# Gated linear attention and hard-swish layer: weight loads on one queue, and another written order of all steps

## The chip, the core and the metric

The kernel runs on one core of a Trainium2 chip. Its time is the device time of one launch in microseconds (us). The times of the kernel before are the median of seven runs; its profile is of one further look at one of these executions, recorded by the hardware profiler.

## The reference

Two blocks are computed one after the other, all in float32 on the chip. The inputs of the second block arrive as float64; the kernel gets their bits and rounds them itself.

```python
# attention: batch 4, heads 8, sequence 768, head size 48
for t in range(S):
    state = alpha[:, :, t, :, None] * state + einsum('bhd,bhe->bhde', k[:, :, t], v[:, :, t])
    y[:, :, t] = einsum('bhd,bhde->bhe', q[:, :, t], state)
# feed forward: x is y as (3072 tokens, 384), w_in (384, 2048), w_out (2048, 384)
h = x @ w_in
g = h * clip(h + 3, 0, 6) / 6
out = g @ w_out
```

## The kernel before

**Tiling.** The 3072 tokens are cut into 24 chunks of 128 tokens (six for each batch), and the chunks are taken in pairs, so there are 12 groups of 256 tokens. The attention of a chunk needs the state that the chunk before has left; the feed-forward part of a group needs the attention of its two chunks. The first two groups (0 and 1) use plain products for the first layer, and group 0 for the second layer too. All other products are done with a scheme of Strassen's kind that needs fewer multiplications: sums of weights are made once on VectorE, sums of activations for each group.

**Weights.** Each matrix is cut into eight slices: 0 to 7 of `w_in`, 8 to 15 of `w_out`. A slice of 768 KB of float64 bits lands in a raw buffer (`load_weight`, L170 to L188; a slice of `w_in` by four transfers of 192 KB, L184, a slice of `w_out` by one, L187). Then five steps make float32 of it: `round_low` (L207, ScalarE), `magnitude` (L217, ScalarE), for slices 0, 1, 2 and 4 also `sign` (L212, ScalarE), `high_bits` (VectorE, L224 and L226 for these slices, L228, L229 and L231 for the others), and `add_low` (L238, GpSimd). Slices share three raw buffers (slices 3 and 4 have room elsewhere), so a later load waits for the `add_low` of an earlier slice.

**Order.** Nothing is scheduled by a tool at build time: the order is written out by hand as one list of 1665 words (the string passed to `run`, L842 on, inside `manual_schedule`). A word such as `sc.1.1.2` calls one step, with the chunk or group first and the PSUM banks to use last. Each engine takes its own instructions strictly in the order of this list, and SyncE its transfers. An instruction that waits holds up all that follow on its engine. The words that matter here:

- `la`, `lk`, `lq`, `lv`: loads of one chunk of alpha, k, q, v, issued by SyncE (L273, L303 and L304 for the first six or eight chunks, as 192 KB and two times 96 KB).
- `w`: `load_weight`; `d1`, `d2`, `dx`, `d3`, `d4`: `round_low`, `magnitude`, `sign`, `high_bits`, `add_low`.
- `ta`, `tk`, `tq` (L314): transposes on TensorE; `ca` (L332, ScalarE) places alpha; `r` (L341, L345) and `p` (L352) are the scans on VectorE; `k`, `q` (L364) the scalings on VectorE.
- `sc` (L408): scores on TensorE; `m` (L416): mask on VectorE; `kb` (L428) and `ck` (L437, ScalarE): k by token; `u` (L494): state update on TensorE; `sm` (L507, L509, VectorE) and `st` (L471, GpSimd): next state; `yi` (L539) and `yx` (L549): the chunk's output on TensorE; `cy` (L557, ScalarE) keeps it.
- `fa`, `fb` (L582): a slice of the first layer for one of the two chunks of group 0; `f` (L571): for a whole group; `fr` (L587, ScalarE) and `fg` (L591, VectorE): its hard swish; `b` (L609): a quarter of the second layer for a chunk of group 0.
- `M` (L693), `n` (L699, ScalarE), `o` (L630 to L634, VectorE), `e` (L587, ScalarE), `h` (L591, VectorE): a product of the first layer, its copy, the sums, and hard swish, from group 2 on. `P` (L796): a product of the second layer, from group 1 on; `s` (L740, L757, VectorE) its sums, `K` (L775), `G` (L809 and L812), `O` (L817) its copies, outputs and stores. `y`, `x`, `xc`: sums of weights and of activations on VectorE.
- `z` (L625): matmuls of the identity into a bank that nobody reads; 29 of them stand in the opening.

**Semaphores of transfers.** The framework gives eight semaphores in turn to the transfers that SyncE and ScalarE issue, so a transfer waits for the landing of the one eight places before it.

The choice of the queue in `load_weight`:

```python
queue = nc.scalar if i < 5 and p > 1 else nc.sync
queue.dma_start(out=to[32 * p : 32 * p + 32], in_=src[p])
```

Of the kernel before, what the change touches and what calls it, by code (L numbers as in the profile page):

```python
# [17 lines left out]
def kernel(  # L18
# [32 lines left out]
    nc = tc.nc  # L51
# [9 lines left out]
    G = 2  # L61
# [66 lines left out]
    st, sm = [], []  # L128
# [43 lines left out]
    def load_weight(i):  # L172
        u = 2 if wide else 1
        dst = weight_dst(i)
        m = dst.shape[1]
        to = raw_of(i).rearrange("p (m n) w -> p m (n w)", m=m) if wide else dst
        if i < NW1:
            n = NSL // KT
            src = moe_w_in[:, u * i * n : u * (i + 1) * n].rearrange(
                "(p t r) f -> p r t f", p=NP, t=KT)  # L180

            for p in range(NP):
                queue = nc.scalar if i < 5 and p > 1 else nc.sync
                queue.dma_start(out=to[32 * p : 32 * p + 32], in_=src[p])  # L184
        else:
            o = (i - NW1) * m * C
            nc.sync.dma_start(  # L187
                out=to, in_=moe_w_out[o : o + m * C, :].rearrange("(f p) n -> p f n", p=C))  # L188
# [476 lines left out]
    for i in range(8):  # L665
        r, o = divmod(i, 3)
# [174 lines left out]
    with tc.manual_schedule():  # L841
        run("""la.0 z.3.5 lv.0.0 lk.1 lq.0 ta.0.0 lv.1.1 z.0.3 ca.0 r.0 lk.0 tk.1.1 la.1 p.0 tq.0.2  # L842
               z.0.8 la.2 q.0 lq.1 tk.0.3 z.0.2 k.0 lv.3.2 ta.1.0 sc.0.2.3 ca.1 la.3 r.1 ta.2.0 w.1
               z.0.3 ca.2 m.0 kb.0.0 z.0.2 ck.0 r.2 tq.1.2 yi.0.3 p.1 z.0.3 lq.2 cy.0 k.1 u.0.0 q.1
               lk.2 ta.3.3 sm.0 sc.1.1.2 ca.3 lk.3 p.2 d1.1 kb.1.0 w.0 m.1 st.1 d2.1 tq.2.3 dx.1
               z.0.1 q.2 yi.1.1 d3.1 tk.2.2 ck.1 yx.1 r.3 u.1.3 lq.3 cy.1 k.2 d4.1 tk.3.0 lv.2.0
               sm.1 sc.2.1.2 k.3 w.3 st.2 fa.1.0 d2.0 m.2 d1.0 kb.2.3 d3.0 fb.1 dx.0 p.3 tq.3.0 w.4
               z.1.2 ck.2 d4.0 q.3 fr.0.1.0 u.2.1 sc.3.2.3 fg.0.1 sm.2 fa.0.1 m.3 st.3 d2.3 d1.3
               kb.3.0 w.5 d3.3 fb.0 ck.3 u.3.1 fr.0.0.1 yi.3.2 d4.3 sm.3 d1.4 fg.0.0 yi.2.3 d2.4 w.2
               dx.4 yx.3 d3.4 yx.2 f.0.3.2 cy.3 d4.4 cy.2 d1.5 la.5 d2.5 f.1.3.3 fr.0.3.0 lq.5 d3.5  # L850
               la.4 d1.2 f.1.4.0 fg.0.3 lv.4.1 d4.5 d2.2 dx.2 w.6 d3.2 tq.5.0 fr.1.3.1 ta.4.1 d4.2
               fr.1.4.0 ta.5.2 fg.1.3 fa.4.1 ca.4 fg.1.4 ca.5 r.4 w.7 fa.2.2 r.5 f.0.5.3 p.4 d2.6
               d1.6 st.4 lq.4 fb.2 fr.0.5.1 d3.6 w.8 f.1.5.0 fr.0.2.0 d1.7 fg.0.5 d4.6 fg.0.2 d2.7
               tq.4.3 fr.1.5.1 f.1.0.3 d3.7 w.9 q.4 d4.7 f.1.6.2 fr.1.0.0 fg.1.5 d2.8 fg.1.0 p.5
               d1.8 w.10 f.1.7.0 d3.8 fr.1.6.1 d2.9 q.5 f.0.7.3 d4.8 d1.9 lk.4 fg.1.6 fr.1.7.0 d3.9
               w.11 f.0.6.2 fr.0.7.1 d2.10 fg.1.7 d4.9 d1.10 fg.0.7 tk.4.1 fr.0.6.0 d3.10 f.1.2.0
               w.12 k.4 d4.10 fb.4 fg.0.6 d2.11 fr.1.2.1 d3.11 sc.4.2.3 w.13 d1.11 fr.0.4.0 f.1.1.3
               fg.0.4 d4.11 m.4 d2.12 d1.12 kb.4.0 lk.5 d3.12 b.1.0.2 fr.1.1.0 ck.4 w.14 fg.1.1
               d4.12 d2.13 fg.1.2 b.0.0.1 d1.13 d3.13 w.15 u.4.1 tk.5.2 d4.13 sm.4 b.1.1 k.5 d2.14
               st.5 d1.14 d3.14 lq.6 sc.5.3.0 yi.4.1 m.5 lq.7 d4.14 b.1.2 d2.15 d1.15 d3.15 la.6  # L860
               yx.4 b.0.1 tq.6 d4.15 lv.5.2 y.6 la.7 b.1.3 y.5 y.1 y.7 lk.7 y.2 y.11 yi.5.2 bo.1 x.0
               so.1 b.0.2 lv.7.0 y.4 y.13 ca.6 yx.5 y.0 b.0.3 cy.5 r.6 la.8 y.3 x.1 s.1.0.0 P.1.0.3
               P.1.1.0 lv.9.1 s.1.1.1 P.1.3.2 cy.4 xc.2.0 s.1.3.2 x.2 s.1.2.3 s.1.4 s.1.5 y.8 xc.2.1
               y.16 K.1.0 P.1.2 bo.0 K.1.2 K.1.1 M.2.15.1 M.2.16 x.3 P.1.4 P.1.5 y.10 y.12 y.9
               xc.2.3 y.15 G.1.1.0 P.1.6 G.1.3.1 xc.2.4 tk.7 lk.9 lk.6 xc.2.5 y.17 xc.2.7 G.1.0.2
               y.19 y.20 xc.2.6 M.2.7.0 n.2.7.8 y.18 M.2.0.3 xc.2.8 M.2.8 G.1.2.3 y.21 y.23 n.2.0.9
               M.2.1 n.2.1.10 o.2.4.0 M.2.17 M.2.2 n.2.2.11 xc.2.9 M.2.18.2 M.2.3 M.2.4 p.6 tk.6 q.6
               ca.7 lq.8 la.9 lv.6.2 lk.8 k.6 sc.6.0.3 xc.2.10 r.7 k.7 xc.2.2 n.2.4.12 o.2.0.0 p.7
               M.2.5 M.2.9 kb.6.2 kb.7.1 n.2.18.13 e.2.0.0 ck.7 tq.7 lq.9 M.2.19 o.2.1.0 M.2.10
               u.7.1 ck.6 u.6.2 O.1.3 m.6 yi.6.0 q.7 y.14 n.2.10.14 sm.6 h.2.0 o.2.5.0 y.22 M.2.11  # L870
               n.2.11.15 o.2.7.0 e.2.5.1 h.2.5 y.24 cy.6 sc.7.3.2 m.7 M.2.12 n.2.12.12 st.7 e.2.1.0
               h.2.1 o.2.6.0 M.2.6.2 e.2.4.1 M.2.13 xc.3.0 n.2.5.14 o.2.3.0 n.2.13.11 o.2.2.0 yi.7.0
               yx.7 cy.7 xc.3.1 xc.3.2 xc.3.3 o.2.2.1 e.2.2.0 M.2.14 xc.3.4 P.2.0.3 o.2.7.1 xc.3.5
               o.2.3.1 M.3.0.1 n.3.0.13 xc.3.7 M.3.7.2 xc.3.6 h.2.4 o.2.6.1 h.2.2 e.2.3.1 h.2.3
               e.2.6.0 M.3.1 P.2.1.0 n.3.7.12 K.2.0 ca.8 tk.8 xc.3.10 xc.3.8 h.2.6 G.2.0.1 n.3.1.11
               e.2.7.1 M.3.2 M.3.8 h.2.7 s.2.0.8 r.8 s.2.1.10 s.2.2.14 k.8 n.3.2.9 M.3.3 M.3.4
               n.3.4.15 o.3.0.0 P.2.3.0 kt.8 s.2.3.8 M.3.5 M.3.9 p.8 lv.10.2 lv.8.0 vh.8 P.2.2
               o.3.1.0 tq.8 s.2.5 q.8 xc.3.9 tk.9 ca.9 M.3.10 K.2.2 P.2.5 n.3.5.10 e.3.0.0 e.3.1.1
               O.1.2 O.1.0 kw.8 lk.10 kr.8 sm.7 r.9 st.8 sc.8.2.3 m.8 s.2.4 h.3.0 K.2.1 n.3.10.8
               M.3.11 M.3.15.1 M.3.16 n.3.11.14 yi.8.0 O.1.1 yx.8 lq.10 la.10 tq.9 lq.11 G.2.2.3  # L880
               O.2.2 k.9 p.9 u.8.1 M.3.12 sm.8 kt.9 kw.9 q.9 h.3.1 M.3.18.0 n.3.18.15 P.2.4 G.2.1.2
               ca.10 sc.9.2.3 m.9 M.3.19 o.3.5.0 n.3.12.9 vh.9 M.3.13 st.9 yi.9.1 yx.9 o.3.4.0
               e.3.4.0 o.3.3.0 M.3.6.0 n.3.13.9 M.3.14 tk.10 o.3.2.0 cy.8 cy.9 xc.4.1 o.3.3.1 xc.4.3
               o.3.2.1 xc.4.4 o.3.6.0 P.2.6 G.2.3.0 vh.10 M.3.17 e.3.2.1 xc.4.5 r.10 xc.4.6 tq.10
               p.10 M.4.0.0 n.4.0.9 P.3.0.3 K.3.0 O.2.1 la.12 kr.9 lv.13.0 lk.11 la.11 xc.4.0 k.10
               q.10 M.4.1 u.9.2 o.3.7.0 o.3.6.1 xc.4.7 xc.4.8 h.3.2 sc.10.3.0 m.10 xc.4.2 h.3.4
               o.3.7.1 ca.11 M.4.7.2 n.4.1.15 e.3.6.1 M.4.2 n.4.2.11 yi.10.1 M.4.3 M.4.4 n.4.7.12
               M.4.8 e.3.5.0 h.3.5 e.3.3.0 n.4.4.8 r.11 h.3.3 P.3.1.1 M.4.5 h.3.6 s.3.0.13 o.4.0.0
# [123 lines left out]
```

## Time and profile before

| what | value |
|---|---|
| median of 7 runs | 547.97 us (547.51 to 551.35) |
| the profiled execution's own time | 549.09 us |
| its span, first to last instruction | 547.3 us |
| granted TensorE clock | 0.999 |
| TensorE matmul, busy | 538.9 us (98%) |
| TensorE weight load, busy | 512.0 us (94%) |
| VectorE, busy | 470.5 us (86%) |
| ScalarE, busy | 203.9 us (37%) |
| GpSimd, busy | 55.6 us (10%) |
| HBM read and written | 43.71 MB and 8.13 MB |
| loads of `w_in` on ScalarE's queue | 10 of 192 KB, median 6.0 us to landing |

The busy time of TensorE bridges short waits, since the ends of matmuls are modelled. Whether it waits is seen in the starts of its instructions: within one kind they follow each other at a fixed distance (a matmul of 128x192 every 163 ns, of 128x128 every 112 ns, of 128x256 every 217 ns), and what exceeds that is lost. The times of single steps below are starts of their first instruction, taken from the timeline by counting the words of the list.

### The profile page before, as it was taken

The page shows a single profiled execution, that of the slowest core. Times are in us where ns is not written, and L with a number is a line of the kernel's source. Part 1 is how long each engine was busy: PE and PEld are TensorE (multiplying, and loading weights), DVE is VectorE, ACT ScalarE, POOL GpSimd, SP SyncE. Part 2 cuts the span into 40 slices and gives each one's busy share as a digit, 9 for nine tenths or more (in the row PEclk, how much of TensorE's full clock was granted, in tenths as well). Part 3 has the DMA queues.
Part 4 walks back from the last instruction along what each step waited for, and adds up shares of the span by engine and source line. Part 5 has one row for each costly group of instructions (what it writes and reads, how often), then busy time and mean ns, then how long its engine had stood idle before and what let it go on. Part 6 is the DMA issues. An engine that isn't in the chain of part 4 may idle for free.

```text
span 547.3 us, 14906 instructions
## 1 busy us (share of the span) xinstructions
PE 538.9 (98%) x6222; PEld 512.0 (94%) x6222; DVE 470.5 (86%) x822; ACT 203.9 (37%) x358; POOL 55.6 (10%) x76
## 2 busy tenths in 40 slices
PE   8999999999999999999999999999999999999996
PEld 8789886699999999999999999999999999999996
DVE  6978997989999999999999998999999796375571
ACT  2487663002543242241432443333243333333330
POOL 3334336000001000000100000000100100000000
PEclk9999999999999999999999999999999999999999
DMA  8998678204414442542443542245143300000000
GB/s 181 193 202 174 207 230 220 63 9 104 94 29 126 111 104 66 140 123 71 126 118 84 151 101 59 79 107 141 38 116 86 91 23 2 1 23 2 23 14 30
DMA packets 98515, 52.82 MB, mean 97 GB/s; under 512 B 51472, under 2 KB 91664, under 8 KB 98448
## 3 DMA queue, kind: packets, MB, share of 16 engines
q1 hardware_dynamic: 97328, 49.91, 36.2%
q10 hardware_dynamic: 1120, 1.97, 1.7%
q8 instruction: 49, 0.80, 0.6%
q14 instruction: 18, 0.15, 0.1%
HBM read 43.71 MB, written 8.13 MB: 95 GB/s over the span
## 4 chain that ended last, share of the span: by engine, by line
PE 94%; issue 2%; DMA 1%; DVE 1%; ACT 1%; ACTq 0%; POOL 0%; POOLq 0%
PE m_ps L796 35%; PE m_ps L693 34%; PE m_ps L571 6%; PE m_ps L609 4%; PE t_ps L549 2%; PE t_ps L383 2%; PE t_ps L529 2%; PE m_ps L582 2%; DMA v<-in_v_dram 1%; PE t_ps L533 1%; PE t_ps L408 1%; PE t_ps L314 1%; PE m_ps L625 1%; PE t_ps L539 1%; PE t_ps L488 1%
## 5 line engine op out<-in xcount | busy, mean ns | idle before, releaser
L796 PE MATMUL m_ps<-w,g_sb 128*128 128x192 f32 x704 | 121.3, 326 | 0.0
L699 ACT COPY g_sb<-m_ps 128x512 f32<-128x512 f32 x110 | 63.5, 585 | 142.8 <-PE m_ps L693 127.9
L796 PEld LDWEIGHTS m_ps<-w,g_sb 128*128 128x128 f32 x704 | 113.8, 190 | 0.4
L796 PE MATMUL m_ps<-rings,g_sb 128*128 128x192 f32 x528 | 91.4, 326 | 0.0
L796 PEld LDWEIGHTS m_ps<-rings,g_sb 128*128 128x128 f32 x528 | 85.4, 190 | 0.1
L693 PE MATMUL m_ps<-xc,w 128*128 128x128 f32 x640 | 82.7, 277 | 0.0
L693 PEld LDWEIGHTS m_ps<-xc,w 128*128 128x128 f32 x640 | 77.9, 192 | 1.6 <-issue 1.2
L587 ACT ACTIVATE r<-g_sb,half 128x512 f32<-128x512 f32 x80 | 56.6, 721 | 40.5 <-DVE g_sb L634 16.1
L591 DVE SCALAR_TENSOR_TENSOR g_sb<-r,g_sb 128x512 f32<-128x512 f32 x80 | 54.4, 693 | 8.1 <-ACT r L587 5.5
L471 POOL TENSOR_TENSOR t<-t,R 128x384 f32<-128x384 f32 x20 | 21.2, 1059 | 337.8 <-DVE t L509 128.7
L693 PE MATMUL m_ps<-xT,raw 128*128 128x128 f32 x400 | 52.3, 277 | 0.0
L693 PEld LDWEIGHTS m_ps<-xT,raw 128*128 128x128 f32 x400 | 48.7, 192 | 0.5
L740 DVE TENSOR_TENSOR g_sb<-g_sb 128x512 f32<-128x512 f32 (+1 forms) x55 | 42.5, 799 | 3.5 <-PE m_ps L796 3.2
L693 PE MATMUL m_ps<-xT,w 128*128 128x128 f32 x320 | 42.6, 277 | 0.0
L693 PEld LDWEIGHTS m_ps<-xT,w 128*128 128x128 f32 x320 | 39.4, 192 | 0.6 <-issue 0.2
L571 PE MATMUL m_ps<-xT,w 128*128 128x256 f32 x144 | 32.3, 381 | 0.0
L693 PE MATMUL m_ps<-xc,raw 128*128 128x128 f32 x240 | 32.1, 277 | 0.0
L341 DVE TENSOR_TENSOR_SCAN R<-t,ones 128x516 f32<-128x516 f32 x24 | 29.9, 1246 | 2.1 <-ACT t L332 2.0
L571 PEld LDWEIGHTS m_ps<-xT,w 128*128 128x128 f32 x144 | 26.9, 190 | 3.7 <-issue 0.2
L630 DVE TENSOR_TENSOR g_sb<-m_ps,g_sb 128x512 f32<-128x512 f32 x30 | 20.5, 683 | 11.3 <-ACT g_sb L699 8.8
L693 PEld LDWEIGHTS m_ps<-xc,raw 128*128 128x128 f32 x240 | 29.6, 192 | 0.4
L352 DVE TENSOR_TENSOR_SCAN P<-t 128x516 f32<-128x516 f32 x24 | 29.6, 1232 | 0.1
(121 smaller groups left out, 745.2 us busy)
## 6 DMA issues: line engine op xcount, KB each, us to landing
raw<-in_moe_w_out_dram SPq DMA_DIRECT2D x8, 768.0 KB, 4.3
out_dram<-oh SPq DMA_DIRECT2D x44, 96.0 KB, 1.8
raw<-in_moe_w_in_dram SPq DMA_DIRECT2D x18, 192.0 KB, 4.2
qq<-in_q_dram SPq DMA_DIRECT2D x36, 96.0 KB, 2.3
aq<-in_alpha_dram SPq DMA_DIRECT2D x36, 96.0 KB, 2.4
kq<-in_k_dram SPq DMA_DIRECT2D x36, 96.0 KB, 2.4
far<-kq SPq DMA_DIRECT2D x13, 256.0 KB, 2.2
kb<-far SPq DMA_DIRECT2D x52, 64.0 KB, 2.0
```

The costliest lines, as they stand in the source:

```text
L341: nc.vector.tensor_tensor_scan(out=reverse(R, n - 1, n), data0=reverse(ax, n, n), data1=reverse(ones, n, n), initial=0.0, op0=ALU.mult, op ...
L352: nc.vector.tensor_tensor_scan(out=P_t[j], data0=aX[j % 2][:, 0:n], data1=ini[j % 2], initial=0.0, op0=ALU.mult, op1=ALU.add)
L471: nc.gpsimd.tensor_tensor(out=st[j % 2], in0=sm[j % 2], in1=R_t[j][:, :, 0:1].to_broadcast([C, NP, 2 * D]), op=ALU.mult)
L571: nc.tensor.matmul(h[:, f], w1[:, kk, o : o + C], xT_t[g][:, kk], start=(kk == 0), stop=(kk == KT - 1))
L587: nc.scalar.activation(out=to, in_=h, func=AF.Relu, bias=half, scale=1.0 / 6.0)
L591: nc.vector.scalar_tensor_tensor(out=to, in0=r, scalar=1.0, in1=h, op0=ALU.min, op1=ALU.mult)
L609: nc.tensor.matmul(o_t[c], gs[0][:, f, c * C : (c + 1) * C], w2[:, f], start=(f == 0), stop=(f == NF - 1))
L630: eng.tensor_tensor(out=out, in0=in0, in1=in1, op=ALU.add if s1 > 0 else ALU.subtract)
L693: nc.tensor.matmul(acc[g][i][:, f * C : (f + 1) * C], spots[w][:, f * C : (f + 1) * C], x_of(g, x), start=(first and f == 0), stop=last, s ...
L699: nc.scalar.copy(out=slots[z], in_=acc[g][i])
L740: nc.vector.tensor_tensor(out=out, in0=in0, in1=in1, op=ALU.subtract)
L796: nc.tensor.matmul(to[g], a, rhs[:, f], start=(first and f == 0), stop=(last and f == HF - 1), skip_group_check=True)
```

## The change

Two things change, and no instruction is added or removed: both lists have the same 1665 words but for banks and slots, and the same 29 idle matmuls.

First, all four transfers of each slice of `w_in` are issued by SyncE; before, ScalarE issued two of the four for slices 0 to 4.

```diff
@@ load_weight
-                queue = nc.scalar if i < 5 and p > 1 else nc.sync
+                queue = nc.sync
```

Second, the list is another permutation. The loads of chunks 0 to 3 are put a little differently, slice 0 is the first to be loaded and made instead of slice 1, and the second layer of group 1 starts before the sums of weights instead of after them. From there on the same kinds of words follow each other, in a different order and on different banks. The opening and the end:

```diff
-        run("""la.0 z.3.5 lv.0.0 lk.1 lq.0 ta.0.0 lv.1.1 z.0.3 ca.0 r.0 lk.0 tk.1.1 la.1 p.0 tq.0.2
-               z.0.8 la.2 q.0 lq.1 tk.0.3 z.0.2 k.0 lv.3.2 ta.1.0 sc.0.2.3 ca.1 la.3 r.1 ta.2.0 w.1
-               z.0.3 ca.2 m.0 kb.0.0 z.0.2 ck.0 r.2 tq.1.2 yi.0.3 p.1 z.0.3 lq.2 cy.0 k.1 u.0.0 q.1
-               lk.2 ta.3.3 sm.0 sc.1.1.2 ca.3 lk.3 p.2 d1.1 kb.1.0 w.0 m.1 st.1 d2.1 tq.2.3 dx.1
-               z.0.1 q.2 yi.1.1 d3.1 tk.2.2 ck.1 yx.1 r.3 u.1.3 lq.3 cy.1 k.2 d4.1 tk.3.0 lv.2.0
-               sm.1 sc.2.1.2 k.3 w.3 st.2 fa.1.0 d2.0 m.2 d1.0 kb.2.3 d3.0 fb.1 dx.0 p.3 tq.3.0 w.4
-               z.1.2 ck.2 d4.0 q.3 fr.0.1.0 u.2.1 sc.3.2.3 fg.0.1 sm.2 fa.0.1 m.3 st.3 d2.3 d1.3
-               kb.3.0 w.5 d3.3 fb.0 ck.3 u.3.1 fr.0.0.1 yi.3.2 d4.3 sm.3 d1.4 fg.0.0 yi.2.3 d2.4 w.2
-               dx.4 yx.3 d3.4 yx.2 f.0.3.2 cy.3 d4.4 cy.2 d1.5 la.5 d2.5 f.1.3.3 fr.0.3.0 lq.5 d3.5
+        run("""la.0 z.3.5 lv.0.0 lk.1 lq.0 ta.0.0 lv.1.1 z.0.3 ca.0 r.0 lk.0 tk.1.1 z.0.2 z.0.8
+               tq.0.2 z.0.2 tk.0.3 p.0 q.0 la.1 ta.1.0 k.0 ca.1 r.1 k.1 sc.0.2.3 m.0 kb.0.0 ck.0
+               z.0.3 z.0.2 la.2 ta.2.0 ca.2 p.1 la.3 lq.1 tq.1.1 z.0.3 ta.3.2 ca.3 kb.1.3 ck.1 lq.2
+               lk.2 tk.2.0 u.0.2 r.2 k.2 q.1 sm.0 p.2 yi.0.3 cy.0 w.0 d1.0 lq.3 lv.2.2 kb.2.0 ck.2
+               z.0.1 sc.1.1.3 m.1 d2.0 dx.0 tq.2.2 q.2 yi.1.0 st.1 yx.1 cy.1 d3.0 u.1.1 sm.1
+               sc.2.3.2 m.2 u.2.0 lk.3 tk.3.1 d4.0 fa.0.0 tq.3.2 fb.0 r.3 k.3 p.3 w.1 d2.1 d1.1 dx.1
+               d3.1 kb.3.3 ck.3 yi.2.1 st.2 yx.2 cy.2 q.3 sc.3.3.2 d4.1 fa.1.1 fb.1 sm.2 st.3 m.3
+               lv.3.0 yi.3.1 yx.3 fr.0.0.0 w.3 d1.3 d2.3 fg.0.0 d3.3 d4.3 w.4 d2.4 d3.4 u.3.0 sm.3
+               la.4 ta.4.2 cy.3 f.1.0.2 d1.4 dx.4 d4.4 ca.4 fr.0.1.1 r.4 st.4 fg.0.1 fr.1.0.0 fg.1.0
...
+               y.21 y.23 xc.2.6 xc.2.7 lq.7 lq.6 lk.7 u.6.1 G.1.0.2 G.1.2.3 sm.6 M.2.15.2 M.2.1
...
-               P.11.2 e.11.2.0 e.11.3.1 h.11.2 h.11.3 P.11.1.3 s.11.5 K.11.1 P.11.4 K.11.2 P.11.5
-               G.11.1.3 G.11.2.2 P.11.6 G.11.3.1 O.11.3 G.11.0.0 O.11.2 O.11.0 O.11.1""")
+               e.11.3.1 h.11.3 P.11.1.0 G.11.0.1 O.11.0 s.11.5 K.11.2 G.10.3.0 K.11.1 P.11.4
+               G.11.1.2 O.11.1 P.11.5 G.11.2.3 P.11.6 G.11.3.1 O.11.3 O.11.2 O.10.3""")
```

The stretch of the new list from the first layer of group 0 to the first Strassen product of group 2, of which the prediction speaks:

```text
...
fg.1.1 d4.11 f.0.7.2 b.1.0.1 b.0.0.3 s.1.0.0 f.0.6.0 tk.5.3 b.1.1 d2.12 d3.12 s.1.1.1 s.1.4
lv.4.1 u.4.0 k.5 sc.5.1.2 fr.0.7.1 fg.0.7 w.14 d1.12 d4.12 w.15 lk.6 d2.13 fr.0.6.0 d1.13 d2.14
d3.13 d4.13 sm.4 st.5 fg.0.6 yi.4.3 yx.4 cy.4 b.0.1 b.1.2 P.1.0.2 b.0.2 la.6 la.7 lv.5.2 m.5
xc.2.0 d3.14 s.1.2.3 s.1.3.2 xc.2.2 yi.5.0 yx.5 d2.15 d3.15 d1.14 d1.15 tk.6 ca.6 la.8 lv.6.0
ca.7 d4.14 d4.15 P.1.1.0 y.1 x.0 y.2 x.1 b.1.3 bo.1 b.0.3 y.6 y.5 s.1.5 y.7 x.2 y.11 y.3 x.3 y.0
cy.5 xc.2.1 K.1.0 P.1.2 K.1.1 so.1 la.9 bo.0 P.1.3.1 K.1.2 P.1.4 P.1.5 y.10 y.8 y.4 xc.2.3 r.6
xc.2.4 y.16 y.13 G.1.1.0 y.9 k.6 kb.6.3 ck.6 P.1.6 G.1.3.1 y.15 y.12 xc.2.5 y.17 y.19 y.20 M.2.0.3
```

## The prediction

> **What bounds the kernel now.** I read the page first, then the windows, the waits and the timeline of the opening, and last the end.
>
> ```profile
> PE 538.9 (98%) x6222; PEld 512.0 (94%) x6222; DVE 470.5 (86%) x822; ACT 203.9 (37%) x358; POOL 55.6 (10%) x76
> DVE  6978997989999999999999998999999796375571
> DMA  8998678204414442542443542245143300000000
> PE 94%; issue 2%; DMA 1%; DVE 1%; ACT 1%; ACTq 0%; POOL 0%; POOLq 0%
> ```
>
> TensorE (PE) is 94% of the chain that ended last. VectorE (DVE) is nearly full up to slice 30 of 40, so it is a second bound close behind. The transfers are busy only at the start. The windows say more:
>
> ```profile
> core 0: us, PE busy (x) PEld busy (x) DVE busy (x) ACT busy (x) POOL busy (x), PEclk, DMA share, GB/s
> 10.00:20.00 10.00, 9.85 (x129) 8.41 (x127) 9.05 (x14) 3.98 (x7) 1.54 (x1) 1.00 0.98 199
> 30.00:40.00 10.00, 8.78 (x191) 8.09 (x189) 8.71 (x15) 7.88 (x10) 4.16 (x3) 1.00 0.92 195
> 40.00:80.00 40.00, 40.00 (x234) 35.87 (x229) 35.64 (x49) 27.88 (x37) 15.76 (x10) 1.00 0.75 202
> 128.60:280.00 151.40, 151.40 (x2008) 146.90 (x2007) 148.19 (x270) 55.62 (x106) 7.64 (x7) 1.00 0.39 99
> ```
>
> From 40 us on PE is full. To see what the opening costs I gave each step its time from the starts in the trace: scores 1.1 us, within 1.0, across 0.75, k by token 0.45, update 0.48, a transpose 0.5, half a slice of the first layer 1.39, a whole one 2.6, a quarter of the second layer 2.69, M 0.917, P 2.6. All useful steps make 529.5 us. "Lost" is the start of a step minus the useful work issued before it. It is 8.2 us at the first scores, 12.6 at the first half slice (26.0 us), 14.1 at `f.0.3` (40.05 us), 13.8 at `M.2.0` (128.6 us) and 13.1 at the last P (540.0 us). So nothing is lost after 40 us: the time is the useful work, plus what is lost in the opening, plus the tail. Where the opening loses:
>
> ```profile
> 23.03 0.48 ACT L557 COPY xT<-t_ps 128x384 f32<-128x384 f32 x1 [0.18 <-PE t_ps L549]
> 25.36 1.76 ACTq L184 DMA_DIRECT2D g_sb<-in_moe_w_in_dram  x2
> 27.29 0.91 ACT L217 ACTIVATE w<-raw 128x768 f32<-128x768 f32 x1 [3.78 <-DMA v<-in_v_dram]
> 30.73 0.68 ACT L437 COPY kb<-t_ps 128x512 f32<-128x512 f32 x1
> 31.46 0.56 PE L494 MATMUL t_ps<-v,kb 128*48 128x48 f32 x16 [1.23 <-ACT kb L437]
> ```
>
> ScalarE (ACT) stands 3.78 us because its own queue holds weight transfers that wait for the landing of earlier ones (here the one of v). Three steps of slice 0 and the copy `ck.2` come behind; `u.2` on PE waits for `ck.2`. At this wait the lost time goes from 12.5 to 14.3 us. The tail:
>
> ```profile
> 542.87 0.32 ACT L809 COPY oh<-m_ps 128x192 f32<-128x192 f32 x1 [9.90 <-issue]
> 543.22 1.80 SPq L817 DMA_DIRECT2D out_dram<-oh  x4
> ```
>
> Four stores are issued after the last copy, one every 0.45 us.
>
> **The Trainium skill.** "DMA: Bandwidth & Descriptors", section "Issuing engines are not separate DMA queues", says that transfers of all issuing engines run on the same 16 DMA engines, so a second issuer saves only issue time. The trace agrees: SyncE alone moved 227 GB/s in the window 5 to 6 us, both queues together 199 from 10 to 20. "SBUF — State Buffer", section "Who interferes with whom", says that VectorE and GpSimd share a port pair, and the later one is blocked. Here a scan beside `add_low` took 1.86 us (at 49.6 us), against 1.23 alone.
>
> **The change part by part.** *Weights by SyncE.* Ten issues of some 0.4 us leave ScalarE, and with them the 3.78 us. SyncE gets ten more issues, 4.3 us in 40 us; it already runs ahead of the landings, which come every 0.93 us per 192 KB, so this costs nothing as long as the DMA engines stay fed. Landing: the first eight loads are the same, the last at 8.4 us. Then come six of 192 KB and slice 0: 8.4 + 6 x 0.93 + 4 x 0.95 = 17.8 us. Before, slice 1 landed at 17.4. The second slice: lq.3, lv.2, lk.3 and four pieces, 17.8 + 3 x 0.93 + 4 x 0.95 = 24.4 us; before 26.1.
>
> *The opening.* I walked the new list by hand, engine by engine, with starts from the trace: a transpose is ready after 0.69 us, r takes 1.35 us on DVE, p 1.2, k or q 0.6, m 1.2, sm 0.75, d3 1.35 (2.35 in the long form), d1 or d2 0.9 on ACT, dx 1.95, d4 1.9 or 1.5 on GpSimd.
>
> | event | before, us | after, worked out |
> |---|---|---|
> | `k.0` on DVE | 9.9 | 10.2 |
> | `sc.1` | 17.7 | 18.9 |
> | first slice: d3 on DVE | 21.4 | 21.9 |
> | first slice: d4 ends | 25.6 | 25.3 |
> | first half slice of the first layer | 26.0 | 25.5 |
> | `u.2` | 31.5 | 24.3 |
> | second slice's first half | 33.05 | 32.15 |
> | first whole slice | 40.05 | 37.7 |
>
> Up to `f.1.0` the new order has issued 26.4 us of useful work, so 11.3 us are lost, where before 14.1 were lost with 25.9 done: 2.8 us less. The gain comes from `u.2`: chunk 2's k is transposed before the weights take ACT, and PE has chunk 2 and 3 at hand while slice 0 and 1 are made. The idle matmuls (29, 6.5 us) stay; they are hidden in gaps that PE has anyway, and cost 0.22 us each where the gap is gone.
>
> *To the first Strassen product.* After `f.1.0` each slice of the first layer is ready before PE comes: the tightest is slice 2, whose d4 ends at 50.1 us against 50.9. DVE then waits for PE once: `s.1.0` writes over a part of g that `b.0.0` still reads, until 80.65 us. From there PE has f 2.6 + six b 16.2 + seven P 18.2 + attention of chunks 4 and 5 with transposes 6.0 = 43.0 us to `M.2.0`. DVE has nineteen y 11.4 + four x 6.8 + four d3 9.4 + six s 4.8 + the rest 10.5 = 42.9 us to `y.20`, which `M.2.0` needs. So `M.2.0` starts at 123.85. Before it was 128.6 with 2.3 us more work in front, which is 126.3 in this order: a gain of 2.45 us, but with DVE only 0.1 us ahead, where before it was 0.9 ahead.
>
> *Group 2 on.* Both engines have the same work in both lists. I compared DVE's sum with PE's at each product. Counted from `M.2.0`, DVE's worst lag before is 0.9 us (`P.2.5`, at `s.2.5`), and it was covered by the lead of 0.9. In the new list it is 0.6 us (`P.2.3`, at `s.2.0`), with 0.1 to cover it: PE waits 0.5 to 0.6 us around 160 us. Then the least margin is near 0, and from 280 us on it grows by several us. The way of k through DRAM keeps 3 us or more of room where DVE is tight (`u.8`, `u.10`). ACT is 37% busy.
>
> *Tail.* Three stores instead of four after the last copy: -0.45 us. The last P steps need sums that DVE has ready in the new order too (0.3 us of room at `P.11.3`).
>
> Sum: -2.45 + 0.6 - 0.45 = -2.3 us. Against the profiled execution: span 547.3 becomes 545.0, own time 549.09 becomes 546.8. Its own time is 1.1 us above the median, so I move the median: 547.97 - 2.3 = 545.7 us.
>
> **Rivals.** *DVE takes the gain (within 0.3%).* DVE's 0.1 us of lead is worth little. Four `add_low` and two state steps of GpSimd fall between 80 and 124 us; if two or three of them stretch a DVE step by 0.6 us, as at 49.6 us, PE waits 1.2 to 1.8 us and the time is 547.2. For it speaks the DVE row, against it that most DVE steps beside an `add_low` show no stretch, and my d3 holds the usual one already.
>
> *The single queue is late (slower).* Slice 0 stands behind six loads on one queue. In the kernel before one issue of k (`lk.3`) held SyncE for 4.0 us (12.85 to 16.86), 2.9 of them put down to `yi.0` on PE. If that falls before slice 0, it lands at 21.8 instead of 17.8, and `d1.0`, with `ck.2` behind it on ACT, starts at 21.8 instead of 18.8. Each us after 18.8 moves the first half slice, and all after it, by one us: +3.0 - 2.3 = +0.7, 548.7. It decides from a landing at 21.1 us on. Against it: when SyncE was held, the DMA engines were full (1.03 and 0.95 in the windows at 12 and 13 us), so the data came at the same rate.
>
> *DVE runs ahead (faster still).* If DVE loses less than I gave it, the 0.6 us vanish and the opening keeps 2.8: 544.6.
>
> *The change moves nothing.* With PE 98% busy the opening could be hidden. It isn't: 14 us are lost there and nowhere given back.
>
> **Numbers.** Two kernels of this kind can be told apart from about 0.3%, which is 1.6 us. Forecast 0.50 (own range 545.0 to 546.8), DVE takes the gain 0.22, single queue late 0.16, DVE ahead 0.12. Below 546.3: about three quarters of the forecast, all of the last, little of the others, 0.56. Slower than 549.6 needs the queue to be late by 4 us or a further stall in the middle: 0.14. The range 543.8 to 549.3 leaves out a tenth on each side: 543.8 if DVE is ahead and DMA feeds ACT earlier, 549.3 for the late queue with more behind it.
>
> **What would show it.** Right: no issue of ScalarE's queue in the opening and no wait of L217 for v; `u.2` near 24 us, the first whole slice of 128x256 near 37.7, `M.2.0` near 124 with `y.20` just before; small PE waits for L757 or L740 near 160 us. Wrong: L207 of slice 0 waits past 19 us for its own transfers; PE waits for DVE between 80 and 130 us; a PE wait for loads or for kb after 150 us, where I see none.

## The result and the profile after

The changed kernel takes 547.73 us (median; 546.66 to 548.81), the kernel before, run beside it, 547.92 us. The ratio is 0.9988, 95% interval 0.9978 to 0.9998. Forecast were 545.7 us, so a gain of 2.3 us; measured are 0.2 us between the medians and 0.7 us by the ratio. The profiled execution took 547.68 us, 0.05 below that median; its span is 545.9 us, 1.4 us shorter than the span of the profile before.

The page of the kernel after, its shares and its chain of work:

```profile
PE 537.6 (98%) x6222; PEld 512.0 (94%) x6222; DVE 476.8 (87%) x822; ACT 203.1 (37%) x358; POOL 51.9 (10%) x76
DVE  6989989999999999999999999999899796465481
PE 83%; DVE 11%; DMA 4%; issue 1%; ACT 0%; POOL 0%; SPq 0%; DVEq 0%; POOLq 0%
```

DVE has come on the chain with 11% (before 1%), and is busy 6.3 us longer with the same 822 instructions. The windows of three of the stretches shown before (columns as there):

```profile
30.00:40.00 10.00, 9.55 (x175) 8.58 (x164) 9.03 (x15) 6.21 (x9) 4.16 (x3) 1.00 1.10 218
40.00:80.00 40.00, 39.03 (x220) 33.80 (x219) 37.10 (x47) 28.05 (x37) 14.78 (x10) 1.00 0.67 183
125.68:280.00 154.32, 154.19 (x2033) 149.85 (x2032) 150.91 (x275) 55.59 (x106) 5.43 (x6) 1.00 0.39 99
```

From 30 to 40 us PE is fuller (9.55 against 8.78). From 40 to 80 us, where it stood full before, 0.97 us are missing. PE's waits in the kernel after say where (engine, line, what it waited for; total, times, longest):

```profile
PE m_ps L571 <- POOL w L238: 1.0, 1, 1.0
PE m_ps L796 <- DVE rings L740: 0.8, 1, 0.8
```

Neither is in the profile before. The first is `f.1.2`, which waits for `d4.2` on POOL (GpSimd), the second is `P.1.2`, which waits for `x.2` on DVE. The timeline of the first (start, duration, engine, line, operation):

```profile
47.91 1.47 POOL L238 TENSOR_TENSOR w<-raw 128x768 int32<-128x768 int32 x1 [2.98 <-DVE raw L231]
48.29 1.63 DVE L224 TENSOR_SCALAR w<-w 128x768 f32<-128x768 f32 x1
...
50.78 1.83 POOL L238 TENSOR_TENSOR w<-w,raw 128x768 int32<-128x768 int32 x1 [1.41 <-ACT raw L207]
51.16 2.55 DVE L352 TENSOR_TENSOR_SCAN P<-t 128x516 f32<-128x516 f32 x1
...
52.67 1.56 PE L571 MATMUL m_ps<-xT,w 128*128 128x256 f32 x6 [0.97 <-POOL w L238]
```

The first two lines are `d4.5` and the start of `d3.2`, side by side: slice 5 goes ahead of slice 2, and beside its `d4` the first instruction of slice 2's `d3` takes 1.63 us, where the other three of L224 in this profile took 0.67 to 0.68. `d4.2` starts at 50.78 and ends at 52.61. In the kernel before this instruction took 1.63 us too (at 46.04, beside the same `d4.5`), but there `f.1.2` came only at 72.3 us.

Further on, two sums of activations of group 1 meet an `add_low` as well (the last two lines are `s.1.2` and `s.1.3` together, and `d4.14`):

```profile
84.07 1.79 POOL L238 TENSOR_TENSOR w<-raw 128x768 int32<-128x768 int32 x1 [4.18 <-ACT w L217]
84.58 2.37 DVE L740 TENSOR_TENSOR g_sb<-g_sb 128x1024 f32<-128x1024 f32 x1
...
95.03 2.56 DVE L740 TENSOR_TENSOR g_sb<-g_sb 128x512 f32<-128x512 f32 x2
95.34 1.69 POOL L238 TENSOR_TENSOR w<-raw 128x768 int32<-128x768 int32 x1 [1.01 <-DVE raw L231]
```

`s.1.4` began at 84.58, inside `d4.12`, and took 2.37 us; in the kernel before, with no `add_low` near, it took 1.22. `s.1.2` began 0.31 us ahead of `d4.14` and took 0.68 us; `s.1.3` began at 95.63, inside it, and took 1.95 us (0.69 before). The profiles of slice2, late_three, relief_after, after_again, fewer_idle, tail and late_three_tail show 2.37 and 1.95 to 1.96 us for these two again. With `r.4` (2.56 us, before 1.86), `p.4` (2.55, before 1.59) and the second instruction of `d3.4` (1.57, before 0.69), all beside an `add_low`, five steps make up 5.0 of DVE's 6.3 us.

ScalarE in the opening of the kernel after:

```profile
19.12 0.92 ACT L207 ACTIVATE raw<-raw 128x768 int32<-128x768 uint32 x1
19.93 0.57 ACT L437 COPY kb<-t_ps 128x512 f32<-128x512 f32 x1
...
24.58 0.94 ACT L217 ACTIVATE w<-raw 128x768 f32<-128x768 f32 x1 [0.79 <-DMA raw<-in_moe_w_in_dram]
```

No transfer stands on ScalarE's queue, the wait of L217 for v is gone, and `ck.2` (L437) is done at 20.5 us instead of 31.4. `u.2` starts at 24.77 us. The tail:

```profile
542.02 0.32 ACT L809 COPY oh<-m_ps 128x192 f32<-128x192 f32 x1 [10.08 <-PE m_ps L796]
542.37 1.30 SPq L817 DMA_DIRECT2D out_dram<-oh  x3
```

Three stores behind the last copy, as counted. So the parts of the change are all there in the trace, and yet the time hardly moved.

### The profile page after: what moved, and what is told of

Its sections match the earlier page's. It is cut to its first block, busy times and chain, and to the rows that moved or that the text cites. A ratio compares the mean times of both kernels' runs of the same rounds, so it can differ in the third digit from the quotient of the medians.

```text
span 545.9 us, 14868 instructions
## 1 busy us (share of the span) xinstructions
PE 537.6 (98%) x6222; PEld 512.0 (94%) x6222; DVE 476.8 (87%) x822; ACT 203.1 (37%) x358; POOL 51.9 (10%) x76
## 4 chain that ended last, share of the span: by engine, by line
PE 83%; DVE 11%; DMA 4%; issue 1%; ACT 0%; POOL 0%; SPq 0%; DVEq 0%; POOLq 0%
PE m_ps L796 33%; PE m_ps L693 32%; PE m_ps L571 3%; DMA raw<-in_moe_w_in_dram 2%; PE t_ps L549 2%; PE t_ps L383 2%; PE m_ps L625 2%; PE t_ps L529 2%; PE t_ps L533 1%; PE t_ps L314 1%; DMA g_sb<-in_moe_w_in_dram 1%; DVE g_sb L740 1%; PE t_ps L488 1%; DVE rings L740 1%; PE t_ps L408 1%; DVE raw L630 1%
## 5 line engine op out<-in xcount | busy, mean ns | idle before, releaser
L693 PE MATMUL m_ps<-xc,w 128*128 128x128 f32 x640 | 83.9, 277 | 0.1
L471 POOL TENSOR_TENSOR t<-t,R 128x384 f32<-128x384 f32 x20 | 18.5, 927 | 331.8 <-DVE t L509 195.7
L740 DVE TENSOR_TENSOR g_sb<-g_sb 128x512 f32<-128x512 f32 (+1 forms) x55 | 44.1, 835 | 0.7 <-PE m_ps L796 0.5
L693 PE MATMUL m_ps<-xT,w 128*128 128x128 f32 x320 | 41.5, 276 | 0.0
L341 DVE TENSOR_TENSOR_SCAN R<-t,ones 128x516 f32<-128x516 f32 x24 | 31.1, 1295 | 4.0 <-ACT t L332 2.9
L630 DVE TENSOR_TENSOR g_sb<-g_sb 128x512 f32<-128x512 f32 x40 | 27.1, 688 | 7.9 <-ACT g_sb L699 7.9
L352 DVE TENSOR_TENSOR_SCAN P<-t 128x516 f32<-128x516 f32 x24 | 30.7, 1280 | 0.2
```

Of the source, the lines that this page charges most:

```text
L341: nc.vector.tensor_tensor_scan(out=reverse(R, n - 1, n), data0=reverse(ax, n, n), data1=reverse(ones, n, n), initial=0.0, op0=ALU.mult, op ...
L352: nc.vector.tensor_tensor_scan(out=P_t[j], data0=aX[j % 2][:, 0:n], data1=ini[j % 2], initial=0.0, op0=ALU.mult, op1=ALU.add)
L471: nc.gpsimd.tensor_tensor(out=st[j % 2], in0=sm[j % 2], in1=R_t[j][:, :, 0:1].to_broadcast([C, NP, 2 * D]), op=ALU.mult)
L630: eng.tensor_tensor(out=out, in0=in0, in1=in1, op=ALU.add if s1 > 0 else ALU.subtract)
L693: nc.tensor.matmul(acc[g][i][:, f * C : (f + 1) * C], spots[w][:, f * C : (f + 1) * C], x_of(g, x), start=(first and f == 0), stop=last, s ...
L740: nc.vector.tensor_tensor(out=out, in0=in0, in1=in1, op=ALU.subtract)
```

## The experiments

"Lost" is used as in the prediction: the start of a step on PE minus the useful work issued before it, with the same durations for both orders. "Before" is the kernel before run on the same chip.

| run | median, us | before, us | ratio, 95% interval | profile's span | lost at M.2.0 |
|---|---|---|---|---|---|
| before_again | 548.19 | 548.45 | 0.9989 (0.9967 to 1.0011) | 547.8 | 14.14 |
| queue_alone | 547.50 | 548.45 | 0.9967 (0.9953 to 0.9981) | 545.7 | 12.15 |
| order_alone | 562.47 | 548.45 | 1.0232 (1.0194 to 1.0270) | 560.9 | 27.24 |
| slice2 | 547.32 | 548.45 | 0.9961 (0.9945 to 0.9978) | 545.0 | 12.00 |
| after_again | 547.81 | 548.10 | 0.9991 (0.9982 to 1.0000) | 545.0 | 12.23 |
| late_three | 546.67 | 548.10 | 0.9967 (0.9954 to 0.9979) | 545.1 | 12.11 |
| tail | 546.59 | 548.10 | 0.9967 (0.9956 to 0.9979) | 545.6 | 13.38 |
| relief_after | 546.94 | 548.10 | 0.9961 (0.9942 to 0.9980) | 544.7 | 11.85 |
| fewer_idle | 548.86 | 548.24 | 1.0014 (1.0000 to 1.0028) | 546.8 | 12.85 |
| late_three_tail | 545.53 | 548.24 | 0.9948 (0.9933 to 0.9963) | 543.4 | 11.25 |
| queue_tail | 546.25 | 548.24 | 0.9958 (0.9944 to 0.9972) | 544.5 | 12.19 |

### Is the profile of the kernel before a typical execution?

The kernel before, unchanged.

> The kernel before, unchanged, for a second profile. Its profiled execution on record was 1.1 us above its median, so a comparison of the two profiles may overstate the gain. Theory A (the opening of the kernel before is steady): useful work lost at the first whole slice of the first layer is 14.1 us again, within 0.3, and the first Strassen product M.2.0 starts at 128.6. Rival B (the profile on record was an unlucky execution): the lost time there is 13 to 13.6 us, M.2.0 starts at 127.5 to 128, and the two kernels are nearer than their profiles say. Ratio 0.998 to 1.002 in both.

The profiled execution took 549.55 us with 14.14 us lost at `M.2.0`: Theory A by the number, but again an execution 1.4 us above the median of its runs (548.19). A third:

> The kernel before again, for a third profile. Both profiled executions of it so far (549.09 and 549.55 us) were 1.0 to 1.5 us above the median of their runs, those of the changed kernel at it or 1.1 us below. Theory A (chance: ScalarE's wait behind its own queue differs from execution to execution): an execution near 548.0 us will show the wait of ScalarE shorter by 1 us or more, or u.2 at 30.5 or earlier, and 12.8 to 13.3 us lost at M.2.0 instead of 14. Rival B (the profiled execution of this kernel is always the slow one, or the extra time comes after M.2.0): 549 us or more again with 14 us lost, or 548 with 14 lost at M.2.0 and less after it.

548.9 us, 13.56 us lost: undecided. Three more, the last two with the same two expectations:

> The kernel before, a fourth profile. Three profiled executions took 549.09, 549.55 and 548.9 us, with 13.6 to 14.1 us lost at M.2.0; the median of the runs is 548.0 to 548.2. Theory A (the wait of ScalarE behind its own queue varies): an execution at 548.2 or less shows no second wait for ck.1 or a shorter one for ck.2, and at most 13.2 us lost at M.2.0. Rival B (the profiled execution of this kernel is always slower): 548.9 or more again, 13.5 us or more lost.

> A fifth profile of the kernel before, with the same two expectations.

> A sixth profile of the kernel before, with the same two expectations.

They took 548.55, 550.97 and 547.55 us, with 13.35, 15.37 and 12.42 us lost at `M.2.0`. The time minus this loss is 535.1 to 535.6 us in all six profiles, so what differs from one execution to the next lies ahead of `M.2.0`. Most of it is ScalarE behind its own queue: between 19 and 28 us it waits there twice ahead of an L217 (for slices 1 and 0), 3.0 us in all in the quickest of the six and 3.4 to 4.8 us in the others. In the slowest (3.9 us) a lower clock of TensorE comes on top; it is shown in the last section. The timeline of ScalarE in the quickest (before_look_4, 547.55 us):

```profile
23.46 1.88 ACTq L184 DMA_DIRECT2D g_sb<-in_moe_w_in_dram  x2
25.52 0.92 ACT L217 ACTIVATE w<-raw 128x768 f32<-128x768 f32 x1 [2.08 <-DMA raw<-in_moe_w_in_dram]
...
28.96 0.70 ACT L437 COPY kb<-t_ps 128x512 f32<-128x512 f32 x1
```

and PE's wait for that copy there:

```profile
PE t_ps L494 <- ACT kb L437: 0.3, 1, 0.3
```

The issues end at 25.3 us instead of 27.1, ScalarE's wait is 2.08 us instead of 3.78, `ck.2` starts at 28.96 instead of 30.73 us, and PE waits 0.3 us for it where it waited 1.2. So Theory A of these profiles holds: the profile that the forecast was built on had 13.81 us lost, and a median execution has 547.92 - 535.3 = 12.6.

### The changed kernel a second time

> The changed kernel, unchanged, for a second profile. In the profile on record its first scores came at 11.45 us, in the four kernels with the same or a similar opening at 10.24 to 10.76. Theory A (slice 2 is late for reasons of its own: a chain of landings, ScalarE, VectorE and GpSimd that does not hang on the first scores): with the scores 0.8 us earlier PE comes to slice 2 0.8 us earlier and waits 0.8 us longer, 1.6 to 1.9 instead of 1.0, and M.2.0 starts at 125.5 to 125.9 again. Rival B (everything moves along): the wait stays at 1.0, M.2.0 starts at 124.9. Ratio to before 0.997 to 0.999.

The first scores came at 10.53 us, `f.1.2` waited 1.0 us again, `M.2.0` started at 124.72 and the time of that execution was 546.74 us. So Rival B: the opening moves along as a whole. What sets the first scores apart is TensorE's pace in the first microseconds. In the profile on record its matmuls of 128x128 follow each other every 213 ns up to 7.2 us, in this one up to 5.2 us, and every 109 to 112 ns from then on. The first transposes, on record and here:

```profile
5.89 1.06 PE L314 MATMUL t_ps<-ident,rings 128*128 128x128 f32 x4
5.56 0.63 PE L314 MATMUL t_ps<-ident,rings 128*128 128x128 f32 x4
```

In the new order `z.0.8` stands ahead of `tq.0`, so a late change of pace reaches the scores: they came at 11.45 and 11.67 us in the two profiles (after and tail) where the change came after 7 us, and at 10.50 to 10.76 in six where it came between 5.0 and 5.7. In the order of the kernel before (eight profiles) they came at 10.21 to 10.66 wherever the change lay between 4.6 and 7.4 us. The record gives the granted clock as 1.00 throughout these microseconds, so what changes the pace is not shown.

Time minus loss at `M.2.0` is 534.5 us in both profiles of this kernel, and its median of 547.73 means 13.2 us lost, as in the profile on record. Set side by side at the medians, `M.2.0` comes with 12.6 us lost before and 13.2 after: in a typical execution the new order is 0.6 us later there, and it gains 0.8 us behind it.

### The two halves of the change

```diff
 # the kernel before, its order kept
-                queue = nc.scalar if i < 5 and p > 1 else nc.sync
+                queue = nc.sync
```

> The order of the kernel before, with the weights of the first five slices all issued by SyncE. Theory A (ScalarE's 3.78 us behind its own queue set ck.2 and with it u.2): the wait vanishes, u.2 starts 1.5 to 3 us earlier than 31.5, lost time at the first whole slice 12.5 to 13.3 instead of 14.1, time 0.8 to 1.5 us below before. Rival B (the landings set the opening, whichever queue issues them): ScalarE waits for slices instead, the first whole slice starts within 0.5 us of 40.05, time within 0.4 us of before.

In the profile the wait of ScalarE is down to 0.92 us, `u.2` starts at 29.75 us (1.5 us earlier than in before_again), and 12.46 us are lost at the first whole slice: Theory A. The median is 0.95 us below before, inside the expected 0.8 to 1.5. Its executions lie between 547.10 and 547.92 us, those of the kernel before on that chip between 547.40 and 552.23. About a third of the gain is that the long executions are gone: 14 of the 48 of the kernel before had a mean granted clock below 0.998 and took 550.0 us or more; the median of the other 34 is 548.12 us, 0.6 above queue_alone.

```diff
 # the changed kernel, its order kept
-                queue = nc.sync
+                queue = nc.scalar if i < 5 and p > 1 else nc.sync
```

> The new order, with half of each of the first five slices issued by ScalarE as before. Theory A (the queue is what the change lives from): ScalarE stands 2 to 4 us behind its own queue again, in the new order too, and the time is 1 to 2 us above the changed kernel. Rival B (the new order alone is what moves u.2, since ck.2 now comes ahead of the weights on ScalarE): u.2 stays at 24.8 within 0.5 us and the time is within 0.5 us of the changed kernel.

Both expectations were far too small: 562.47 us, 14.7 us above the changed kernel. PE's waits, and ScalarE's ahead of the first:

```profile
PE m_ps L571 <- ACT xT L557: 5.7, 1, 5.7
PE t_ps L539 <- ACT kb L437: 5.5, 1, 5.5
```

```profile
24.55 0.88 ACT L207 ACTIVATE raw<-raw 128x768 int32<-128x768 uint32 x1 [6.01 <-DMA raw<-in_moe_w_in_dram]
25.33 0.57 ACT L437 COPY kb<-t_ps 128x512 f32<-128x512 f32 x1
```

The new order has `w.0` behind `cy.0` in ScalarE's program. So ScalarE issues its two pieces of slice 0 at 18.06 and 18.49 us, the second lands at 24.44 (all four by 18.25 in the changed kernel), `d1.0` stands for it, and `ck.2` stands behind `d1.0`. The section "Issuing engines are not separate DMA queues" of "DMA: Bandwidth & Descriptors" in the Trainium skill, cited in the prediction, counts only the time to issue as what a second issuer can change; here it changed when the transfer starts, since the issue has its place among ScalarE's other work, and that decides. Not all of the 14.7 us is waiting: the clock fell as well (last section). The new order needs the single queue; the single queue doesn't need the new order.

### Slice 2

```diff
-w.5 d2.5 d1.5 d3.5 d4.5 f.1.3.3 fr.1.3.1 fg.1.3 w.2 d1.2 d2.2 dx.2 d3.2 d4.2
+w.2 d1.2 d2.2 dx.2 d3.2 d4.2 f.1.3.3 fr.1.3.1 fg.1.3 w.5 d2.5 d1.5 d3.5 d4.5
```

> The changed kernel, with the five steps of slice 2 (load, round_low, magnitude, sign, high_bits, add_low) ahead of those of slice 5, whose product comes 6 us later on PE. Theory A (what PE loses while it waits for slice 2 goes through to the end): no wait of f.1.2, M.2.0 starts 0.8 to 1.1 us earlier than 125.68, time 0.8 to 1.1 us below the changed kernel, 546.7. Rival B (VectorE is the bound at M.2.0 and after it): PE stands for VectorE instead, at P.1.2, at M.2.0 or between 130 and 280 us, and the time is within 0.3 us of the changed kernel.

`f.1.2` no longer waits. Two other waits of PE are there instead:

```profile
PE m_ps L796 <- DVE rings L740: 0.7, 1, 0.7
PE t_ps L428 <- DVE k L364: 0.7, 1, 0.7
```

The first is `P.1.2` as before. The second is new: `kb.4` waits for `k.4`, which has not moved. Against after_again, whose first scores come at the same time, 1.0 us less is lost at `f.1.2` (11.12 and 12.12), but only 0.2 less at `M.2.0` (12.00 and 12.23) and nothing less at the end. The median is 0.4 to 0.5 us below the two of the changed kernel, on other chips. Between the two theories: most of the 1.0 us gained at `f.1.2` is lost again at the next waits for VectorE.

### Slice 2, x.2 and kb.4 together

```diff
 # with slice 2 ahead of slice 5, as above
-kb.4.3 fa.2.1
+fa.2.1 kb.4.3
-b.1.3 bo.1 b.0.3 y.6 y.5 s.1.5 y.7 x.2 y.11
+b.1.3 bo.1 b.0.3 x.2 y.6 y.5 s.1.5 y.7 y.11
```

> The changed kernel with three arrivals mended: slice 2 ahead of slice 5, x.2 ahead of y.6 (P.1.2 waits for it), kb.4 after fa.2 on PE (it waits for k.4). Theory A (VectorE has 43 us of work from s.1.0 to y.20, as much as PE has from b.0.0 to M.2.0, so it gives back only what PE's start of b.0.0 gives): the 0.7 us at kb.4 come through, of the 0.7 us at P.1.2 at most 0.3; lost time at M.2.0 11.1 to 11.5 instead of slice2's 12.0, time 0.5 to 0.9 below slice2. Rival B (PE's own waits are all there is): both come through, lost time at M.2.0 10.6, time 1.4 below slice2.

The waits at `P.1.2` and for `k.4` are gone. But from `b.0.0` to `M.2.0` PE took 46.01 us (78.59 to 124.60), in after_again 46.02: all of the 0.9 us that PE lost at `P.1.2` came back within the next 15 us, in two other waits of PE in late_three:

```profile
PE t_ps L428 <- DVE k L364: 0.4, 1, 0.4
PE m_ps L693 <- DVE raw L630: 0.2, 1, 0.2
```

These are `kb.6` for `k.6`, and `M.2.0` for a sum in raw that VectorE makes just ahead of it; counted by the spacing of PE's starts they cost 0.54 and 0.37 us. That is Theory A's picture, VectorE's sum of work. What `kb.4` gave stays, as Theory A also said: from `f.1.0` to `M.2.0` 0.14 us of the loss are given back here, where slice2 loses 0.74 and after_again 1.11 us. The loss at `M.2.0` is not the expected 11.1 to 11.5, because this execution lost 1.0 us more in the opening than slice2 (12.25 and 11.26 at `f.1.0`). The median is 1.1 us below the changed kernel on the same chip.

### Work taken from VectorE

```diff
-        minus(*[(t[3], b[1, 1], b[0, 1]), ..., (t[4], b[1, 0], t[2])][i])
+        minus(*[v[:, 0:1] for v in [(t[3], b[1, 1], b[0, 1]), ..., (t[4], b[1, 0], t[2])][i]])
```

> The changed kernel with the four subtractions of combine_w2 cut to one of their eight rows, so the rest of the sums of the second layer's weights is left out; this takes about 6 us from VectorE between 103 and 115 us. Theory A (VectorE's pace holds PE at P.1.2 and at some products between 124 and 280 us): the 0.8 us at P.1.2 vanish, lost time at 257 us falls from 14.2 to 12.9 or less, time 1.2 us or more below the changed kernel. Rival B (what PE loses after 124 us is not VectorE's, only the wait at P.1.2 is): lost time still grows by 1.0 us from M.2.0 to 257 us, time 0.6 to 0.9 below.

From `b.0.0` to `M.2.0` PE took 45.04 us, 1.0 less than in after_again: here the wait at `P.1.2` is gone for good. From `M.2.0` to `M.6.0` it took 153.14 us, in after_again 153.02. So between these two VectorE holds nothing up, and Rival B is right; the median is 0.87 us below the changed kernel, 0.6 to 0.9 expected.

### The stores at the end

```diff
 # the changed kernel
-P.11.6 G.11.3.1 O.11.3 O.11.2 O.10.3
+P.11.6 O.11.2 O.10.3 G.11.3.1 O.11.3
 # queue_tail: the kernel before with the single queue
-P.11.6 G.11.3.1 O.11.3 G.11.0.0 O.11.2 O.11.0 O.11.1
+P.11.6 G.11.0.0 O.11.2 O.11.0 O.11.1 G.11.3.1 O.11.3
```

> The changed kernel with the stores O.11.2 and O.10.3, ready long before, ahead of the last copy and its store. Theory A (one store behind the last copy instead of three, 0.45 us each): span and time 0.9 us below the changed kernel. Rival B (the last store's landing of about 1.8 us ends the kernel, the stores issued behind it only overlap): within 0.3 us.

> The order of the kernel before with the weights on SyncE's queue, and G.11.0.0, O.11.2, O.11.0 and O.11.1 ahead of the last copy, so that one store comes behind it instead of four. Theory A (0.45 us for each store that no longer waits behind the last copy): 547.5 - 1.3 = 546.2 us, below the changed kernel. Rival B (the new order has something that this one lacks beside its shorter tail): not below 546.9.

The end of tail's timeline:

```profile
540.51 2.84 SPq L817 DMA_DIRECT2D out_dram<-oh  x3
542.67 0.32 ACT L809 COPY oh<-m_ps 128x192 f32<-128x192 f32 x1 [10.08 <-PE m_ps L796]
```

Two stores go out before the last copy and one behind it. From the end of that copy to the end of the span are 2.6 us with one store behind it (tail and queue_tail), 3.6 with three (after_again) and 4.1 with four (queue_alone), so about 0.5 us for each store. The medians fall by 1.22 us (two stores; 0.9 expected) and, from queue_alone to queue_tail, which ran on different chips, by 1.25 us (three; 1.3 expected). Theory A in both. The median of queue_tail, which lacks the new order, is 1.5 us below the changed kernel's and 0.3 us below that of tail, which has it, on another chip.

### Fewer idle matmuls

```diff
-z.0.2 z.0.8 tq.0.2 z.0.2 tk.0.3
+z.0.2 tq.0.2 z.0.2 tk.0.3 z.0.5
```

> The changed kernel with z.0.8 taken from ahead of tq.0 on PE, and five of its idle matmuls put behind tk.0. Theory A (the idle matmuls ahead of tq.0 are not hidden: VectorE stands 0.7 to 1.9 us for tq.0, and all behind moves along): q.0 on VectorE at 8.2, the first scores at 9.7 to 10.0 instead of 10.5 to 11.7, and the time 0.8 to 1.5 us below the changed kernel's 547.8. Rival B (landings of the weights or of chunk 1 set the opening anyway): the first half slice still starts at 24.9 to 26 and the time stays within 0.3 us.

Neither came: the time is 548.86 us, 1.05 above the changed kernel on another chip. `q.0` was at 8.3 us as expected, but `tk.0` then stood 0.35 us for its transfer (landed at 8.59), and the ten idle matmuls that I had put behind it (`z.0.5`, 9.13 to 10.24) held `ta.1` and with it the scores, which came at 10.77. PE stood once more later, at a place where it does not stand in the profiles of after, after_again, slice2 and late_three:

```profile
182.15 0.27 PE L385 MATMUL t_ps<-q,k 48*64 48x64 f32 x1 [0.76 <-issue]
```

The scores are 0.24 us later than in after_again, so the loss of time is not theirs. This pause in the middle of `sc.9` costs 1.0 us in this profile, counted by the spacing of PE's starts. Why it is there, and whether it is there in every execution, stays open. Five of its 22 executions also had a mean granted clock below 0.998 and took 550.9 to 551.6 us; those of the changed kernel never did.

### The parts that help, together

> The kernel with the three arrivals mended (slice 2, x.2, kb.4), and the stores O.11.2 and O.10.3 ahead of the last copy. Theory A (the two parts do not touch each other): 546.67 - 1.0 = 545.7 us, 0.5 to 0.9 us below either alone. Rival B (the store order was worth 1.2 us by chance of the runs): 546.2 or more.

545.53 us (545.18 to 545.72), 1.14 below late_three: Theory A. It beats both kernels, the one before by 0.52% (interval 0.37 to 0.67%).

## Why the prediction was wrong

The direction and the mechanisms of the opening were right, the size was not. The sum was -2.45 at `M.2.0`, +0.6 behind it, -0.45 at the tail; measured are about -0.2 between the medians (the interval of the ratio reaches from -0.1 to -1.2 us). By step:

- **"So I move the median": +1.2 us.** This is the step that failed first. The forecast took the difference of one profiled execution and put it on the median. But 13.81 us lost at `M.2.0` were that execution's; six profiles range from 12.4 to 15.4, and the median has 12.6. The extra was the very wait that the change takes away, 3.78 us here and 2.08 in before_look_4, so it was counted as gain for all executions. That the profiled execution stood 1.1 us above the median was noted, and should have been taken off the gain instead of carried along.
- **"After f.1.0 each slice is ready before PE comes": +1.1 us.** Slice 2 was forecast to end at 50.1 us and ended at 52.61. Its `d3` was behind `r.4` (2.56 us beside an `add_low`, 1.35 reckoned) and the `d3` of slice 5, and beside that slice's `d4`. The Trainium skill's "SBUF — State Buffer", section "Who interferes with whom", was cited for a scan, with the later instruction blocked; the trace after agrees: L224 took 1.63 us where it began 0.38 us after an `add_low`, and 0.68 where it began 0.22 us ahead of one (37.03 us); a scan that began inside one took 2.55 (1.23 alone). slice2 shows that the wait goes away with the order.
- **"PE has 43.0, DVE 42.9": the balance came out nearly right, by two errors that cancel.** The forecast has both sums begin at 80.65 us (and puts `M.2.0` at 123.85, where 80.65 + 43.0 is 123.65). In the trace VectorE's begins 1.1 us before TensorE's: `s.1.0` starts at 81.13 us, `b.0.0` is done at 82.22. And DVE took 44.2 us to the end of `y.20` (125.36), 1.3 more than reckoned, since `s.1.4` and `s.1.3` beside an `add_low` took 2.4 us more than in the kernel before. PE took 43.5 us to `M.2.0` (125.68), 0.8 of it the wait at `P.1.2`. From `s.1.4` to `x.2` DVE didn't stand, so without the two stretches `x.2` would have been ready some 2.4 us earlier and this wait would not be there (an estimate; no run took the stretches alone away). late_three shows that the wait taken away by order comes back as others, relief_after that it goes with VectorE's work. So it adds nothing to the sum beside the bound that was forecast, VectorE at `M.2.0`.
- **The opening: +0.8 us.** Forecast were 11.3 us lost at `f.1.0`, the profile shows 12.06, the second one 11.12. The first scores came at 11.45 and 10.53 us, as TensorE's pace rose at 7.2 or 5.2 us, and all behind them moved along. "Idle matmuls are hidden in gaps" is false ahead of `tq.0` (VectorE waited 1.63 and 0.71 us for it); fewer_idle did not turn that into time.
- **The stall of 0.6 us at 160 us did not come: -0.6.** From `M.2.0` to the last P both kernels lose the same within 0.2 us, and relief_after rules VectorE out up to `M.6.0` (278 us). What the profile before shows as DVE near full was not a bound in that stretch.
- **Tail: -0.45 right**: from the end of the last copy to the end of the span are 4.07 us before and 3.56 after, and the two store experiments agree.

Put together: -2.3, +1.2 for the base, +1.8 for what is lost at `M.2.0` after (13.2 instead of 11.36), and -0.9 behind it (a gain of 0.8 measured, a loss of 0.15 forecast), makes -0.2.

The gain was put down to the order ("chunk 2's k is transposed before the weights take ACT"). queue_alone corrects that: the queue brings the gain, and the order on balance adds none. Of the rivals, "DVE takes the gain" named the right outcome, within 0.3%, and a mechanism that is there: two DVE steps between 80 and 124 us were stretched by an `add_low`, by 1.15 and 1.27 us, and PE waited 0.8 us for DVE; a third stretch struck slice 2 at 48 us. But its hit is in part luck, since it moved the median as the forecast did and so lacks the 1.2 us of the base. The single queue was not late: slice 0 landed at 18.25 us (17.8 forecast), slice 1 at 24.5 (24.4).

## What to carry to other kernels

Before a gain is read from a wait, see whether the wait is as long in a median execution: where the profiled execution is above the median, the wait you want to take away may be what put it there. Transfers on a compute engine's queue are issued only when that engine's program gets to them, so moving steps around such an issue can cost more than the steps themselves. When two engines have the same sum of work between two points where one waits for the other, mending a wait inside that stretch moves it to the next one (`P.1.2`); take work off the second engine, or leave it. A wait outside the stretch (`f.1.2`, `kb.4`, the stores) can be mended by order. And a sum of work misses what begins beside what: look up which steps of VectorE begin while GpSimd works.

## What the runs showed of the hardware

A wait of 5.5 us on PE had a second price. order_alone in windows of 2 us (the third number from the right is the granted clock):

```profile
20.00:22.00 2.00, 0.48 (x4) 0.23 (x3) 1.81 (x3) 0.00 (x0) 0.47 (x1) 1.00 1.11 233
22.00:24.00 2.00, 0.00 (x0) 0.00 (x0) 0.00 (x0) 0.00 (x0) 0.00 (x0) 0.68 1.13 201
...
26.00:28.00 2.00, 2.00 (x40) 1.85 (x44) 1.23 (x2) 2.00 (x2) 0.00 (x0) 0.50 0.84 123
28.00:30.00 2.00, 2.00 (x44) 1.51 (x38) 0.16 (x2) 1.02 (x2) 1.38 (x1) 0.61 0.05 9
30.00:32.00 2.00, 2.00 (x38) 1.82 (x37) 1.74 (x4) 0.00 (x0) 1.29 (x2) 1.00 0.78 215
```

PE stood from 20.5 to 25.9 us. In windows of 0.5 us the clock is at half from 22.7 us on, 2.2 us after PE had stopped, and full again from 29.6, 3.6 us after it had started. The Trainium skill's "TensorE: Matmul & The Clock Gate", "Part 1: The HAM clock gate", says: half rate after an idle window of some 3.4 us, full rate after as long a busy one. The way back agrees; the fall came sooner. In before_look_3 (550.97 us) PE waited for `ck.1` from 22.8 to 24.4 us only, and the granted clock was still 0.54, 0.50, 0.50 and 0.76 in the four microseconds from 26 us on. In before_look_1 PE stood just as long at that place (1.6 us) and the clock stayed at 1.00. So the clock can fall after a stand shorter than the page's window, and the measurement decides; that this stand was what made it fall is not shown. It is no single case: of the 121 executions of the kernel before that ran beside the experiments on three chips, 26 had a mean granted clock below 0.998, and they took 549.6 to 552.2 us; the others took 547.2 to 550.8. Of the 22 executions of queue_alone and the 47 of the changed kernel none had. So with ScalarE's queue goes not only the wait behind it, but also the lower clock in about a fifth of the executions.
